# Whole float32 scores for the first batch, and GpSimd for the token differences of layer 2, in an attention and two-layer kernel

## The chip, the cores and the metric

The kernel runs on one core of a Trainium2 chip. The metric is device time in microseconds (us) from the profiler's clock. Five engines work side by side, each with its own queue of instructions in a fixed order: TensorE (PE; its weight loads are shown as PEld), VectorE (DVE), ScalarE (ACT), GpSimd (POOL) and SyncE (SP), which here only issues transfers (DMA).

## The reference

```python
scores = (q @ k^T) / 8                          # 4 batches, 8 heads, 576 tokens, 64 wide
scores = where(scores >= max(scores) - tau, scores, -1e9)
attn = softmax(scores);  x = (attn @ v), heads side by side      # 2304 x 512
h = x @ w1_in;  x = (h * clip(h + 3, 0, 6) / 6) @ w1_out          # 512 -> 2048 -> 512
h = x @ w2_in;  out = (h - tanh(h)) @ w2_out                      # 512 -> 2048 -> 512
```

All inputs and the output are float32. The threshold keeps only scores within tau = 0.02 of a row's maximum, so scores have to be nearly as exact as float32.

## The kernel before

**Products.** TensorE's fast formats carry fewer bits than float32. The kernel therefore splits each float32 operand into a high and a low part and multiplies the parts, in float32r (written fp32r; the profile shows its matmuls as f32) for attention and layer 1 and in float16 for layer 2.

**Attention.** The work is cut into 144 units, 36 for each batch. Most units are 128 queries of one head against all 576 keys; per pair of heads one leftover unit holds the last 64 queries of both heads (576 = 4 x 128 + 64). For a unit `softmax` (line 662) issues the scores into a bank of PSUM (ring `R_s`, two banks), the row maximum on VectorE (L683), the exponential on ScalarE (L685), and the mask times exponential on VectorE (L694), which is the last reader of the bank. Then the result is split into two float16 parts (L699 ScalarE, L705 GpSimd), transposed by a DMA (L708), and four units later multiplied with v (L731).

**Scores with parts.** `k_round` (line 564) transposes k (L561, leftover rows L577). ScalarE writes the high part of one head into rows 0 to 63 of a tile `ks` and of the other head into rows 64 to 127 (L584); VectorE subtracts and writes the low parts into the other half (L586). So the 128 rows of one head hold its high and low parts, one above the other. For q each raw block stands twice side by side in `qr` (a copy by GpSimd, L554), so that its transpose is the same 64 rows twice; ScalarE makes the high part (L591) and VectorE the low part (L593), in the tile `q`, or `qs` for leftover queries. A unit's scores are then, for the high and the low part of q, two matmuls of 288 keys each, four in all, which add up all four products of parts. A leftover unit has two heads and eight matmuls; zeros in `qs` keep the heads apart.

**Weights.** While batch 0 runs, the first half of layer 1's weights is brought from 64-bit form to parts: sixteen pieces, each with a load (L406, L411), a ScalarE step (L414), four VectorE steps (L418, L420, L423, L426), ScalarE's high part (L448) and GpSimd's low part (L451). The pieces are called `ai` and `ao` when they go into matmuls.

**Layers.** Layer 1 takes each batch in two parts (`layer1`, line 819; matmuls at L489 and L850), between the attention units of later batches; its second half of hidden columns follows after all attention, from about 485 us (`hidden`, L489 with tiles `xh`, `bw`). Layer 2 starts at about 720 us. It multiplies blocks of tokens by blocks of weights in a seven-product scheme (Strassen-Winograd), which needs differences of token blocks. `tokens` (line 1315) loads a pair of blocks (L1322), makes four differences T1 to T4 for each of four pairs and one, T5, for the single last block (L1351, 17 in all), and splits each piece into two float16 parts (L1274 ScalarE, L1276 VectorE). It is called once for each pair, in the first of four rounds; later rounds use the same pieces.

**Order.** Every instruction is a task with an engine, an estimated duration and a priority (`add`). `Plan.issue` (line 103) runs a list schedule with these durations, and the order in which it starts the tasks is the order of each engine's queue. A different duration or engine in one place can therefore change the order elsewhere. The transfers are tasks as well, on SyncE's queue.

Of the kernel before, what the change touches and what calls it, by code (L numbers as in the profile page):

```python
# [9 lines left out]
F32 = mybir.dt.float32  # L10
# [5 lines left out]
ACTF = mybir.ActivationFunctionType  # L16
# [14 lines left out]
class Buf:  # L31


    def __init__(self, ring, prev):
        self.ring, self.prev, self.users, self.writers = ring, prev, [], []
        self.tile, self.slot, self.ends = None, None, []

    @property
    def t(self):
        if self.tile is None:  # L40
            self.tile = self.ring.make() if self.slot is None else self.ring.make(self.slot)
        return self.tile


# [156 lines left out]
def attention_moe_moe_kernel(  # L201
# [29 lines left out]
    nc = tc.nc  # L231
    B, H, S, D = q.shape
# [5 lines left out]
    NC = S // 128  # L238
    SM = NC * 128
    LF = S - SM  # L240
    NP = H // 2
    NT = B * S
    SH = S // 2
    ORDER = [0, 2, 1, 3]
    scale = 1.0 / float(D) ** 0.5
# [10 lines left out]
    add = plan.add  # L256

    LAG = 4
    STEP, SLOW, KNEE = 3.0, 0.8, 4
    LK, LQ, LV, LD = 5, 3, 1, 4  # L260
    XL, FO = 1, 7
# [3 lines left out]
    PVK, GK, RK = -4.0, -6.0, -1.0  # L265
# [9 lines left out]
    ST, SB, CS = 4.0, 2.0, 0.0  # L275
# [11 lines left out]
    tau_b = const.tile([128, 4], F32, name="tau_b")  # L287
# [233 lines left out]
    def load_q_left(b, half, key):  # L521

        t = QL[b, half] = R_ql.new()
        hs = slice(half * NP, (half + 1) * NP)
        for r in range(2):
            add("dma", 0.65, key, lambda r=r: nc.sync.dma_start(
                out=t.t[:, :, r, :], in_=q[b, hs, SM:S, :].rearrange("h p d -> p h d")), w=[t], xfer=0.37, slack=SB)

    def load_k(b, j, key):
        t = KR[b, j] = R_kr.new()  # L530
        add("dma", 0.6, key, lambda: nc.sync.dma_start(
            out=t.t, in_=k[b, 2 * j:2 * j + 2, 0:SM, :].rearrange("h (p c) d -> p h c d", c=NC)), w=[t], xfer=0.88, slack=SB)

# [11 lines left out]
    def load_q(b, g, j, key, eng="dma"):  # L545

        t = QR[b, g, j] = R_qr.new()
        queue = nc.sync if eng == "dma" else nc.scalar
        for i in range(2):
            add(eng, 0.47, key, lambda i=i: queue.dma_start(  # L550
                out=t.t[:, i, :, 0, :],
                in_=q[b, 2 * j + i, 0:SM, :].rearrange("(p c) d -> p c d", c=NC)[:, 2 * g:2 * g + 2, :]), w=[t], xfer=0.37, slack=SB)
        copy = lambda r: t.t[:, :, :, r, :].rearrange("p h c d -> p (h c) d")
        add("pool", 0.5, key + 4, lambda: nc.gpsimd.tensor_copy(copy(1), copy(0)), r=[t], w=[t])  # L554

    def transposes(ps, srcs):

# [6 lines left out]
    def k_round(b, j, part, key):  # L564

        if part == 0:
            KS[b, j] = R_k.new()
        ks, tp, kr, kl = KS[b, j], R_tp.new(), KR[b, j], KL[b]
        half = (slice(0, 64), slice(64, 128))
        n = (SM // 2, LF)[part]  # L570

        def tr():
            if part == 0:
                transposes(tp.t, [(kr.t[:, i, c:c + 2, :], 0) for i in range(2) for c in (0, 2)])
            else:
                for i in range(2):
                    nc.tensor.transpose(tp.t[0:64, i * LF:(i + 1) * LF], kl.t[:, 2 * j + i, :], ident[0:LF, 0:LF])  # L577

        add("pe", 2 * n * 0.00085, key, tr, r=[kr] if part == 0 else [kl], w=[tp, ks])
        for x in range(2 - part):  # L580
            cols = slice(x * n, (x + 1) * n) if part == 0 else slice(SM, S)
            out = lambda up, cols=cols: ks.t[half[up], :, cols]
            src = lambda x=x: tp.t[half[x], 0:2 * n].rearrange("p (i n) -> p i n", i=2)
            hi = add("act", t_act(2 * n), key + RK, lambda x=x, out=out, src=src: nc.scalar.activation(  # L584
                out=out(x), in_=src(), func=ACTF.Copy), r=[tp], w=[ks])
            add("dve", t_dve(2 * n), key + RK, lambda x=x, out=out, src=src: nc.vector.tensor_tensor(  # L586
                out=out(1 - x), in0=src(), in1=out(x).bitcast(F32), op=ALU.subtract), r=[tp], w=[ks], after=[hi])
# [8 lines left out]

    def q_round(b, g, j, key):

        qr, tp, qt = QR[b, g, j], R_tp.new(), R_q.new()
        add("pe", 4 * 0.11, key, lambda: transposes(  # L600
            tp.t, [(qr.t[:, i, c, :, :], 0) for i in range(2) for c in range(2)]), r=[qr], w=[tp, qt])
        q_split(qt, tp, lambda x: qt.t[:, x], 256, key)
        QT[b, g, j] = qt

    def q_left_round(b, j, key):

        ql, tp, qt = QL[b, 2 * j // NP], R_tp.new(), R_qs[j % 2].new()
        add("pe", 2 * 0.06, key, lambda: transposes(
            tp.t, [(ql.t[:, (2 * j + i) % NP, :, :], LF) for i in range(2)]), r=[ql], w=[tp, qt])
        q_split(qt, tp, lambda x: qt.t[:, x].rearrange("p (i n) -> p i n", n=LF)[:, 0:3:2, :], LF, key)  # L610
        QT[b, "l", j] = qt
# [50 lines left out]
    def softmax(u, key):  # L662
# [8 lines left out]
        s = lambda: ps.t[:, :, 0:SH]  # L671
        ex = lambda: e.t[:, n, :].rearrange("p (a s) -> p a s", a=2)

        def scores():
            ops = [(queries(b, g, j, x, c, part), KS[b, j].t[:, x % 2]) for x in hs for part in range(2)]
            for i, (l, ks) in enumerate(ops):
                for half in range(2):
                    nc.tensor.matmul(  # L678
                        ps.t[:, half, 0:SH], l, ks[:, half * SH:(half + 1) * SH], start=i == 0, stop=i == len(ops) - 1,
                    )  # L680

        add("pe", 0.53 * len(hs), key, scores, r=[KS[b, j], QT[b, g if h is not None else "l", j]], w=[ps])
        add("dve", 0.69, key, lambda: nc.vector.tensor_reduce(  # L683
            out=z.t[:, 0:1], in_=s(), axis=AX.XY, op=ALU.max, negate=True), r=[ps], w=[z])
        exp = add("act", 0.66, key, lambda: nc.scalar.activation(  # L685
# [179 lines left out]
    with tc.manual_schedule():  # L865
# [94 lines left out]
        start = 0.0  # L960
# [353 lines left out]
        def tokens(p, key, after_y, after):  # L1314
# [26 lines left out]
            def make(name, key):  # L1341

                for o, a, b in sums:
                    if o == name and o not in made:
                        made.add(o)
                        make(a, key)
                        make(b, key)
                        t = R_c.new()
                        src[o] = ((lambda t=t: t.t.rearrange("p (k n) -> p k n", k=2)), t)
                        (fo, bo), (fx, bx), (fy, by) = src[o], src[a], src[b]  # L1350
                        add("dve", t_dve(2 * n), key, lambda: nc.vector.tensor_tensor(  # L1351
                            out=fo(), in0=fx(), in1=fy(), op=ALU.subtract), r=[bx, by], w=[bo], after=after, slack=CL)

            four = lambda i: x.t[:, i, 0:2].rearrange("p a (k n) -> p (a k) n", k=2)
# [242 lines left out]
```

## Time and profile before

| | us |
|---|---|
| median of 3 runs | 1088.65 (1088.2 to 1093.36) |
| the profiled execution | 1088.51 |
| its span, first to last instruction | 1086.7 |
| around the span | 1.8 |
| TensorE busy in the span | 1015.0 (93%) |
| VectorE busy | 847.6 (78%) |
| ScalarE busy | 718.6 (66%) |
| GpSimd busy | 339.0 (31%) |

A share of the whole span is a mean over stages with different limits, so the stage tables below say more than this table does. The granted TensorE clock is given as a share of 2.4 GHz; it has two levels, 0.5 (1.2 GHz) and 1.0.

### The profile page before, as it was taken

To read this page: it belongs to the slowest core of one execution; us is meant where nothing else is said; L and a number is where in the kernel's file an instruction comes from. 1 tells how busy PE (TensorE), PEld (TensorE's weight loads), DVE (VectorE), ACT (ScalarE), POOL (GpSimd) and SP (SyncE) were. 2 spreads that over 40 slices of the span, in tenths; PEclk is the share of its full clock that TensorE was granted. 3 is DMA by queue.
4 is the path that set the end of the run, shared out by engine and by line. 5 is a ranking of instruction groups with operands and counts; after the bars stand their busy time and mean duration, and the time that the engine had idled before them with its cause. 6 is when DMAs were issued, how large, how long until landed. Compare 5 with 4: busy or idle time off the path is not lost.

```text
span 1086.7 us, 23294 instructions
## 1 busy us (share of the span) xinstructions
PE 1015.0 (93%) x8984; PEld 838.6 (77%) x8984; DVE 847.6 (78%) x1630; ACT 718.6 (66%) x1312; POOL 339.0 (31%) x353
## 2 busy tenths in 40 slices
PE   5668799999999899988999999999999999999998
PEld 4557788998999799978988888876676666666664
DVE  5889977687869788758797778889976796784564
ACT  6867979687967786645675566756755675574332
POOL 2656757666855675623000000000001111121000
PEclk8668899999999989998999999999999999999999
DMA  7899688967899989978657755432333866573335
GB/s 184 165 222 213 132 159 182 196 132 158 187 181 192 205 175 216 219 159 261 201 173 257 253 199 185 165 108 97 107 117 118 208 131 117 126 127 51 87 92 142
DMA packets 285007, 179.27 MB, mean 165 GB/s; under 512 B 202976, under 2 KB 257760, under 8 KB 284896
## 3 DMA queue, kind: packets, MB, share of 16 engines
q1 hardware_dynamic: 279088, 168.07, 61.0%
q0 software_dynamic: 5184, 9.44, 6.5%
q8 instruction: 71, 1.16, 0.5%
q14 instruction: 40, 0.33, 0.1%
q10 hardware_dynamic: 624, 0.26, 0.1%
HBM read 89.13 MB, written 46.14 MB: 124 GB/s over the span
## 4 chain that ended last, share of the span: by engine, by line
PE 58%; DVE 4%; ACT 1%; DMA 1%; issue 0%; SPq 0%; ACTq 0%; DVEq 0%
PE ya L489 24%; PE m L489 16%; PE h L489 10%; PE m L850 3%; PE s L678 2%; PE tp L731 1%; DMA y<-y 1%; PE h L850 1%; PE m L476 0%; DVE x L1276 0%; DMA st<-in_moe_w_in_dram 0%; DVE xh L1048 0%; DVE t L803 0%; PE tp L561 0%; DVE y L1175 0%
## 5 line engine op out<-in xcount | busy, mean ns | idle before, releaser
L705 POOL TENSOR_TENSOR pp<-e,pp 128x128 f16<-128x128 f32 (+3 forms) x156 | 181.1, 1182 | 120.3 <-issue 54.1
L489 PE MATMUL ya<-wo,g 128*128 128x512 f16 x864 | 205.4, 379 | 1.0 <-DVE g L813 0.6
L489 PEld LDWEIGHTS <-wi 128*128 128x128 f16 x1536 | 150.0, 98 | 40.4
L1416 POOL DMA_DIRECT2D po<-o x36 | 31.2, 876 | 459.7 <-ACT o L1410 459.7
L489 PEld LDWEIGHTS <-g 128*128 128x128 f16 x864 | 84.1, 98 | 79.3 <-DVE g L813 1.1
L683 DVE TENSOR_REDUCE z<-s 128x1 f32<-128x576 f32 x144 | 107.9, 753 | 45.4 <-PE s L678 44.7
L694 DVE SCALAR_TENSOR_TENSOR e<-s,z,e 128x576 f32<-128x576 f32 x144 | 115.8, 811 | 22.1 <-ACT e L685 17.1
L678 PE MATMUL s<-ks,q 128*128 128x288 f32 x512 | 105.9, 337 | 20.9 <-DVE e L694 20.1
L685 ACT ACTIVATE e<-s,z 128x576 f32<-128x576 f32 x144 | 105.0, 739 | 26.6 <-DVE z L683 20.3
L489 PE MATMUL m<-xT,ai 128*128 128x256 f32 (+1 forms) x720 | 112.8, 301 | 1.8 <-DVE st L426 0.6
L678 PEld LDWEIGHTS s<-ks,q 128*128 128x128 f32 x512 | 82.4, 212 | 29.4 <-DVE e L694 13.4
L489 PEld LDWEIGHTS m<-xT,ai 128*128 128x128 f32 x720 | 99.3, 190 | 3.7 <-DVE st L426 1.1
L489 PE MATMUL ya<-g,bo 128*128 128x256 f16 x864 | 101.1, 273 | 0.5 <-DVE g L813 0.5
L731 PE MATMUL tp<-vt,pt 128*128 128x65 f16 (+1 forms) x2240 | 88.4, 199 | 8.5 <-ACT q L591 2.4
L489 PE MATMUL m<-x,wi 128*128 128x256 f16 x768 | 95.2, 273 | 0.0
L731 PEld LDWEIGHTS <-pt 128*128 128x128 f16 (+1 forms) x2240 | 79.8, 104 | 16.7 <-DMA pt<-pp 6.0
L1381 ACT ACTIVATE t<-t,hid_s 128x512 f32<-128x512 f32 x72 | 51.6, 718 | 62.0 <-DVE t L1372 61.4
L489 PEld LDWEIGHTS <-bo 128*128 128x128 f16 x864 | 84.1, 98 | 10.6 <-issue 0.9
L489 PEld LDWEIGHTS <-bw 128*128 128x128 f16 x864 | 84.1, 98 | 10.4 <-issue 0.4
L813 DVE SCALAR_TENSOR_TENSOR g<-g,t 128x512 f16<-128x512 f16 x108 | 73.8, 686 | 20.7 <-ACT g L809 20.2
L809 ACT ACTIVATE g<-t 128x512 f16<-128x512 f32 x108 | 67.0, 624 | 33.7 <-DVE t L1383 26.0
L699 ACT ACTIVATE pp<-e 128x1152 f16<-128x1152 f32 (+1 forms) x80 | 85.1, 1064 | 5.0 <-DVE e L694 4.7
(177 smaller groups left out, 1878.0 us busy)
## 6 DMA issues: line engine op xcount, KB each, us to landing
st<-in_moe_w_in_dram SPq DMA_DIRECT2D x40, 512.0 KB, 5.0
st<-in_moe_w_out_dram SPq DMA_DIRECT2D x40, 512.0 KB, 4.4
xf<-xs SPq DMA_DIRECT2D x18, 512.0 KB, 5.2
y<-y SPq DMA_DIRECT2D x18, 512.0 KB, 3.8
po<-o POOLq DMA_DIRECT2D x36, 256.0 KB, 4.2
xs<-xT SPq DMA_DIRECT2D x8, 640.0 KB, 4.9
y<-ys SPq DMA_DIRECT2D x9, 512.0 KB, 5.9
po<-o SPq DMA_DIRECT2D x18, 256.0 KB, 2.0
```

The lines of the kernel that those rows point to most:

```text
L489: nc.tensor.matmul(ps, l[a], r[b], start=first and t == 0 and i == 0, stop=last and t == 2 and i == n - 1,)
L678: nc.tensor.matmul(ps.t[:, half, 0:SH], l, ks[:, half * SH:(half + 1) * SH], start=i == 0, stop=i == len(ops) - 1,)
L683: add("dve", 0.69, key, lambda: nc.vector.tensor_reduce(out=z.t[:, 0:1], in_=s(), axis=AX.XY, op=ALU.max, negate=True), r=[ps], w=[z])
L685: exp = add("act", 0.66, key, lambda: nc.scalar.activation(out=ex(), in_=s(), func=ACTF.Exp, bias=z.t[:, 0:1]), r=[ps, z], w=[e])
L694: add("dve", 0.74, key, lambda: nc.vector.scalar_tensor_tensor(out=ex(), in0=s(), scalar=z.t[:, 1:2], in1=ex(), op0=ALU.is_ge, op1=ALU.mul ...
L699: high = add("act", t_act(w * S, sbuf=True), key, lambda: nc.scalar.activation(out=pp.t[:, 0:w, 0:S], in_=e.t[:, 0:w, :], func=ACTF.Copy), ...
L705: add(eng, dur, key, lambda src=src, dst=dst, queue=queue: queue.tensor_tensor(out=pp.t[:, 0:w, dst], in0=e.t[:, 0:w, src], in1=pp.t[:, 0: ...
L731: nc.tensor.matmul(pv.t[0:m, w_ * (D + 1):(w_ + 1) * (D + 1)], pt.t[:, n, blk, rows], vv, start=o == 0, stop=o == len(ops) - 1)
L809: hi = add("act", t_act(n, sbuf=True), key, lambda: nc.scalar.activation(out=gh(), in_=t(), func=ACTF.Copy, scale=GS2 if far else 1.0), r= ...
L813: go = lambda: nc.vector.scalar_tensor_tensor(out=gl(), in0=gh(), scalar=1.0 / GS2, in1=t(), op0=ALU.mult, op1=ALU.subtract)
L850: prev = [add("pe", t_mm(n, 1), kd, lambda p=p, l=l, r=r, m=m, s=s, ps=ps: nc.tensor.matmul(ps.t[:, 0:n], W["o", m].t[:, l, s], r[m].t[:, ...
L1381: add("act", t_act(2 * NB, sbuf=True, scalars=True), key, lambda: nc.scalar.activation(out=s_(), in_=h.t, func=ACTF.Tanh, scale=c), r=[h], ...
```

## The change

For batch 0 (`WHOLE = (0,)`) q and k are no longer split. One ScalarE copy takes the transposed k of a head pair into a float32 tile, head 0 in rows 0 to 63 and head 1 in rows 64 to 127; q likewise, with the scale. A unit's scores are two float32 matmuls of 288 keys, with 64 rows of q and k. For a leftover unit the two heads' queries stand in different rows and columns of the tile `q`, the rest of which VectorE clears, and the 128 rows of both heads are multiplied at once. The loads of k and of the raw q put the two heads' 64 columns side by side for each block, so that one transpose serves both heads; k comes in two transfers in place of one, the leftover q in one in place of two, and the doubling copies of q are not made. In `tokens` the differences move from VectorE to GpSimd.

```diff
+    WHOLE = (0,)
@@ load_q_left, load_k, load_q
+        if b in WHOLE:
+            add("dma", 0.65, key, lambda: nc.sync.dma_start(
+                out=t.t.rearrange("p h r d -> p (h r) d")[:, 0:NP, :], in_=q[b, hs, SM:S, :].rearrange("h p d -> p h d")),
+                w=[t], xfer=0.37, slack=SB)
+            return
...
+        for i in range(2 if b in WHOLE else 0):
+            add("dma", 0.5, key, lambda i=i: nc.sync.dma_start(
+                out=cells(t)[:, :, i, :], in_=k[b, 2 * j + i, 0:SM, :].rearrange("(p c) d -> p c d", c=NC)), w=[t], xfer=0.44, slack=SB)
...
+        if b in WHOLE:
+            for i in range(2):
+                add(eng, 0.47, key, lambda i=i: queue.dma_start(
+                    out=pairs_of(t)[:, :, i, :],
+                    in_=q[b, 2 * j + i, 0:SM, :].rearrange("(p c) d -> p c d", c=NC)[:, 2 * g:2 * g + 2, :]), w=[t], xfer=0.37, slack=SB)
+            return
@@ new
+    def pairs_of(t):
+        return t.t.rearrange("p i c r d -> p (i c r d)")[:, 0:4 * D].rearrange("p (c i d) -> p c i d", c=2, i=2)
+    def cells(t):
+        return t.t.rearrange("p i c d -> p (i c d)").rearrange("p (c i d) -> p c i d", c=NC, i=2)
+    def whole(ring, tag):
+        t = ring.new()
+        t.make = lambda: at_p.tile([128, 2, S] if tag == "ks" else [128, 2, 2, 256], F32, tag=tag, name=tag + "w", bufs=ring.n)
+        return t
@@ k_round
+        if b in WHOLE:
+            w = (SM, LF)[part]
+            def turn_whole():
+                if part:
+                    nc.tensor.transpose(tp.t[:, 0:LF], kl.t[:, 2 * j:2 * j + 2, :].rearrange("p i d -> p (i d)"), ident[0:LF, 0:LF])
+                for x, c in enumerate(() if part else ORDER):
+                    nc.tensor.transpose(tp.t[:, x * 128:(x + 1) * 128], cells(kr)[:, c].rearrange("p i d -> p (i d)"), ident)
+            add("pe", w * 0.00085, key, turn_whole, r=[kl if part else kr], w=[tp, ks])
+            add("act", t_act(w), key + RK, lambda: nc.scalar.activation(
+                out=ks.t[:, 0, part * SM:part * SM + w], in_=tp.t[:, 0:w], func=ACTF.Copy), r=[tp], w=[ks])
+            return
@@ q_round, q_left_round
+            add("pe", 2 * 0.11, key, lambda: [nc.tensor.transpose(
+                tp.t[:, c * 128:(c + 1) * 128], pairs_of(qr)[:, c].rearrange("p i d -> p (i d)"), ident) for c in range(2)],
+                r=[qr], w=[tp, qt])
+            add("act", t_act(256, scalars=True), key + RK, lambda: nc.scalar.activation(
+                out=qt.t[:, 0, 0], in_=tp.t[:, 0:256], func=ACTF.Copy, scale=tau_b[:, 2:3]), r=[tp], w=[qt])
...
+            clear = add("dve", 0.1, key, lambda: nc.vector.memset(qt.t[:, 0, 1, 0:2 * LF], 0.0), w=[qt])
+            add("pe", 0.06, key, lambda: nc.tensor.transpose(...), r=[ql], w=[tp, qt])
+            for i in range(2):
+                half = slice(i * 64, i * 64 + 64)
+                add("act", t_act(LF, scalars=True), key + RK, lambda i=i, half=half: nc.scalar.activation(
+                    out=qt.t[half, 0, 1, i * LF:(i + 1) * LF], in_=tp.t[half, 0:LF], func=ACTF.Copy, scale=tau_b[half, 2:3]), r=[tp], w=[qt], after=[clear])
@@ softmax
+        def scores_whole():
+            rows = slice(0, 128) if h is None else slice(h % 2 * 64, h % 2 * 64 + 64)
+            qt, ks = QT[b, g, j].t, KS[b, j].t
+            l = qt[:, 0, 1, 0:2 * LF] if h is None else qt[rows, 0, 0, c % 2 * 128:c % 2 * 128 + 128]
+            for half in range(2):
+                nc.tensor.matmul(
+                    ps.t[:, half, 0:SH], l, ks[rows, 0, half * SH:(half + 1) * SH], start=True, stop=True)
-        add("pe", 0.53 * len(hs), key, scores, r=[...], w=[ps])
+        add("pe", 0.98 if b in WHOLE else 0.53 * len(hs), key, scores_whole if b in WHOLE else scores, r=[...], w=[ps])
@@ tokens
-                        add("dve", t_dve(2 * n), key, lambda: nc.vector.tensor_tensor(
+                        add("pool", t_pool(2 * n), key, lambda: nc.gpsimd.tensor_tensor(
                             out=fo(), in0=fx(), in1=fy(), op=ALU.subtract), r=[bx, by], w=[bo], after=after, slack=CL)
```

## Rows read from the trace of the kernel before

**Rows 1.** Busy time by stage: PE, PEld, DVE, ACT, POOL; clock, DMA share, GB/s

```profile
10.00:97.00 87.00, 59.89 (x458) 50.24 (x457) 75.21 (x126) 66.83 (x128) 51.70 (x47) 0.67 0.87 195
97.00:136.00 39.00, 31.33 (x367) 28.59 (x364) 37.27 (x65) 34.82 (x76) 27.61 (x28) 0.91 0.78 159
136.00:480.00 344.00, 329.46 (x3705) 312.97 (x3702) 263.41 (x514) 259.18 (x496) 213.88 (x217) 0.99 0.87 180
...
700.00:760.00 60.00, 57.06 (x450) 43.56 (x448) 55.34 (x119) 41.33 (x68) 0.00 (x0) 1.00 0.29 102
760.00:1087.00 327.00, 321.91 (x2158) 210.81 (x2155) 230.28 (x424) 173.22 (x295) 31.25 (x36) 1.00 0.50 118
```

**Rows 2.** Waits of PE in the first 97 us: total, times, longest

```profile
PE s L678 <- DVE e L694: 13.5, 12, 2.6
```

**Rows 3.** Timeline of the start: start, length, instruction, idle before it

```profile
5.13 1.09 PE L561 MATMUL tp<-ident,kr 128*128 128x128 f32 x4 [5.13 <-DMA kr<-in_k_dram]
...
6.26 1.20 ACT L584 ACTIVATE ks<-tp 64x512 fp32r<-64x512 f32 x2 [3.21 <-PE tp L561]
...
7.49 1.39 DVE L586 TENSOR_TENSOR ks<-tp,ks 64x512 fp32r<-64x512 f32 x2 [2.94 <-ACT ks L584]
...
10.51 1.31 PE L678 MATMUL s<-ks,q 128*128 128x288 f32 x4
```

**Rows 4.** Transfers issued in the first 97 us: size, median us to landing

```profile
kr<-in_k_dram SPq DMA_DIRECT2D x7, 256.0 KB, 4.2
...
qr<-in_q_dram SPq DMA_DIRECT2D x16, 64.0 KB, 3.8
```

**Rows 5.** Groups on DVE by form, first 140 us: busy us, mean ns

```profile
L586 DVE TENSOR_TENSOR ks<-tp,ks 64x512 fp32r<-64x512 f32 x12 | 8.3, 689 | 4.1 <-ACT ks L584 3.8
L593 DVE SCALAR_TENSOR_TENSOR q<-tp,tau_b,q 128x512 fp32r<-128x512 f32 x10 | 7.4, 745 | 0.7 <-ACT q L591 0.6
...
L586 DVE TENSOR_TENSOR ks<-tp,ks 64x128 fp32r<-64x128 f32 x6 | 1.7, 284 | 0.7 <-ACT ks L584 0.5
L593 DVE SCALAR_TENSOR_TENSOR qs<-tp,tau_b,qs 128x128 fp32r<-128x128 f32 x4 | 1.4, 341 | 0.0
```

**Rows 6.** Timeline of PE: scores and transposes at both clock levels

```profile
20.55 1.30 PE L678 MATMUL s<-ks,q 128*128 128x288 f32 x4 [0.95 <-DVE e L694]
...
93.44 2.29 PE L678 MATMUL s<-ks,qs 128*128 128x288 f32 x8
...
100.57 0.66 PE L561 MATMUL tp<-ident,qr 128*128 128x128 f32 x4
...
102.17 0.79 PE L678 MATMUL s<-ks,q 128*128 128x288 f32 x4 [0.94 <-DVE e L694]
```

**Rows 7.** Groups on PE by form, first 140 us: line 628

```profile
L628 PE MATMUL tp<-vs,ones 128*128 128x1 f32 x10 | 2.2, 288 | 2.4 <-ACT vt L626 2.0 <-DVE m L418 0.4
```

**Rows 8.** Groups on PE by form, first 97 us: scores of full units

```profile
L678 PE MATMUL s<-ks,q 128*128 128x288 f32 x96 | 28.9, 450 | 11.3 <-DVE e L694 10.9
```

**Rows 9.** Busy time in two stretches, columns as in rows 1

```profile
91.00:94.00 3.00, 2.86 (x10) 2.18 (x11) 3.00 (x5) 2.62 (x5) 0.87 (x2) 0.50 1.19 272
105.00:125.00 20.00, 19.03 (x229) 17.76 (x230) 19.10 (x35) 18.13 (x44) 15.64 (x17) 1.00 0.93 194
```

**Rows 10.** Line 1351 alone: ns min/median/max, first and last start

```profile
L1351 DVE TENSOR_TENSOR c<-y x9: 673/681/691, 714.9 to 771.0; 128x512 f32<-128x512 f32 x9
```

**Rows 11.** Groups on POOL by form, first 140 us: the low parts of weights

```profile
L451 POOL TENSOR_TENSOR ai<-st,ai 128x512 fp32r<-128x512 f32 x8 | 10.4, 1304 | 4.6 <-ACT ai L448 4.6
```

**Rows 12.** Timeline, 490 to 497 us: DVE beside POOL

```profile
491.25 0.75 DVE L1128 SCALAR_TENSOR_TENSOR bw<-st,wmax,bw 128x512 f16<-128x512 f32 x1
...
494.52 2.45 POOL L816 TENSOR_TENSOR gl<-t,gh 128x320 fp32r<-128x320 f32 x2 [7.76 <-ACT gh L809]
...
495.14 1.09 DVE L1128 SCALAR_TENSOR_TENSOR bw<-st,wmax,bw 128x512 f16<-128x512 f32 x1 [0.19 <-ACT bw L1126]
```

**Rows 13.** Timeline of PE, 712 to 765 us: layer 2's first piece

```profile
720.53 1.47 PE L489 MATMUL m<-x,wi 128*128 128x256 f16 x12
```

More of the change, by code (lines that the diff above doesn't have):

```diff
@@ L35, in __init__ @@
         self.ring, self.prev, self.users, self.writers = ring, prev, [], []
-        self.tile, self.slot, self.ends = None, None, []
+        self.tile, self.slot, self.ends, self.make = None, None, [], None
     @property
@@ L40, in t @@
         if self.tile is None:
-            self.tile = self.ring.make() if self.slot is None else self.ring.make(self.slot)
+            self.tile = self.make() if self.make else self.ring.make() if self.slot is None else self.ring.make(self.slot)
         return self.tile
@@ L566, in k_round @@
         if part == 0:
-            KS[b, j] = R_k.new()
+            KS[b, j] = whole(R_k, "ks") if b in WHOLE else R_k.new()
         ks, tp, kr, kl = KS[b, j], R_tp.new(), KR[b, j], KL[b]
@@ L570, in k_round @@
         n = (SM // 2, LF)[part]
+        if b in WHOLE:
+            w = (SM, LF)[part]
[7 more added lines that the diff above has]
+                out=ks.t[:, 0, part * SM:part * SM + w], in_=tp.t[:, 0:w], func=ACTF.Copy), r=[tp], w=[ks])
+            return
         def tr():
@@ L597, in q_round @@
     def q_round(b, g, j, key):
+        if b in WHOLE:
+            qr, tp, qt = QR[b, g, j], R_tp.new(), whole(R_q, "q")
+            add("pe", 2 * 0.11, key, lambda: [nc.tensor.transpose(
[3 more added lines that the diff above has]
+                out=qt.t[:, 0, 0], in_=tp.t[:, 0:256], func=ACTF.Copy, scale=tau_b[:, 2:3]), r=[tp], w=[qt])
+            QT[b, g, j] = qt
+            return
         qr, tp, qt = QR[b, g, j], R_tp.new(), R_q.new()
@@ L605, in q_left_round @@
     def q_left_round(b, j, key):
+        if b in WHOLE:
+            ql, tp, qt = QL[b, 2 * j // NP], R_tp.new(), QT[b, 1, j]
+            clear = add("dve", 0.1, key, lambda: nc.vector.memset(qt.t[:, 0, 1, 0:2 * LF], 0.0), w=[qt])
+            add("pe", 0.06, key, lambda: nc.tensor.transpose(
+                tp.t[:, 0:LF], ql.t.rearrange("p h r d -> p (h r d)")[:, 2 * j % NP * D:(2 * j % NP + 2) * D], ident[LF:2 * LF, LF:2 * LF]),
+                r=[ql], w=[tp, qt])
+            for i in range(2):
+                half = slice(i * 64, i * 64 + 64)
+                add("act", t_act(LF, scalars=True), key + RK, lambda i=i, half=half: nc.scalar.activation(
+                    out=qt.t[half, 0, 1, i * LF:(i + 1) * LF], in_=tp.t[half, 0:LF], func=ACTF.Copy, scale=tau_b[half, 2:3]), r=[tp], w=[qt], after=[clear])
+            QT[b, "l", j] = qt
+            return
         ql, tp, qt = QL[b, 2 * j // NP], R_tp.new(), R_qs[j % 2].new()
@@ L680, in scores @@
                     )
-        add("pe", 0.53 * len(hs), key, scores, r=[KS[b, j], QT[b, g if h is not None else "l", j]], w=[ps])
+        add("pe", 0.98 if b in WHOLE else 0.53 * len(hs), key, scores_whole if b in WHOLE else scores, r=[KS[b, j], QT[b, g if h is not None else "l", j]], w=[ps])
         add("dve", 0.69, key, lambda: nc.vector.tensor_reduce(
```

## The prediction

> **What bounds the kernel now.** I read the stage table first [rows 1], because the change touches two places only. From 760 us on TensorE is busy for 321.9 of 327 us at full clock: nothing off TensorE can be worth much there. In the 60 us from 700 to 760, where layer 2 starts, 60 - 57.1 = 2.9 us are idle. From 136 to 480 us TensorE is busy 329.5 of 344 us at a granted clock of 0.99. The opening is different. Between 10 and 97 us, which is batch 0 before the first matmul of layer 1, TensorE is busy 59.9 of 87 us, and that at a mean clock of 0.67, while VectorE is busy 75.2 (86%), ScalarE 66.8 and the DMA engines 0.87. VectorE is the fullest engine, but not a full one. The view of TensorE's waits for the first 97 us says how it acts on TensorE [rows 2]: 13.5 us in 12 waits of the score matmuls for line 694, the masked exponentials that free a score bank. Between 97 and 136 us VectorE is busy 37.3 of 39 us and TensorE 31.3, so 7.7 us of TensorE are idle there.
>
> The order of instructions on each engine is fixed when the program is built, and nothing in it refers to the time on the chip. So a microsecond gained before 136 us is kept to the end as long as TensorE stays full behind it, and a microsecond of TensorE work added after 97 us is mostly paid.
>
> **The start (term A).** The timeline of the start [rows 3] is a chain: transposes of k until 6.2, two ScalarE copies until 7.5, two VectorE subtractions until 8.9, then q's and the leftover rows of k, and the first scores at 10.51. With whole numbers one copy of k (0.6) and one of q (taken as 0.5) end near 7.4, the leftover's transpose and copy near 8: about -2.4 us. Against it stands the load of k, now two issues with short runs. A 256 KB load of k lands in 4.2 us and a 64 KB load of q, whose runs are as short, in 3.8 [rows 4], so halves of 128 KB should land at much the same time. I take -2.0.
>
> **VectorE, batch 0.** Removed: 8 subtractions of 64x512 at 0.689, 4 of 64x128 at 0.284, 8 of q at 0.745 and 4 of the leftover q at 0.341 [rows 5]: 5.5 + 1.1 + 6.0 + 1.4 = 14.0 us. Added: four clears of 128 elements, bounded below by nothing and above by the 0.284 of a small subtraction; I take 0.17, 0.7 in all. Net -13.3 us, of which 2.4 lie before 10 us (already in A), about 10 between 10 and 97, and 1 after. ScalarE loses four of its eight 512-wide copies of k and half the width of q's; GpSimd loses the eight copies that doubled q. Neither is the fullest engine, so these count as nothing; if VectorE were no cover, ScalarE's 66.8 us would be the next limit.
>
> **TensorE, batch 0.** Before, a unit's scores are four streams of 288 columns: hi and lo of k lie one above the other in 128 rows, so two passes (hi and lo of q) by two halves form all four partial products. Such a unit takes 1.30 us at the low clock and 0.79 at the high one [rows 6]. After, k fills only 64 rows and nothing is stacked. No row shows a wide float32 product; the nearest is line 628, where 5 float32 products stand as 10 matmuls and 10 weight loads [rows 7], that is two of each per product. Low end: the two products of a unit are then four streams as now, and cost nothing more. High end: the four partial products, no longer stacked, need four streams for each half, eight in all. That has a row: the leftover units already run eight streams, in 2.29 us at the low clock [rows 6]; at the high clock, by the same ratio, 1.3 to 1.4. I take the high end, since four partial products in 64 rows cannot be had in fewer streams: +0.95 us a unit at the low clock, +0.5 at the high one. The Trainium skill (FP8 and Floating Point Precision, TensorE Precision Notes) counts a true float32 product as four passes through the array, which would give the same eight streams; no run here shows it yet. There are 32 such units, 24 of them before 97 us (96 matmuls, four a unit [rows 8]); the four leftover units have eight streams before and after. Savings: two transposes instead of four for each of eight q rounds, half of 1.09 us at the low clock and of 0.66 at the high one [rows 3, 6], so 0.5 or 0.3 each.
>
> **10 to 97 us (term B).** If VectorE's occupancy sets the stretch, 65.2 us of work at the same 86% take 75.5 us: -11.5. If TensorE sets it, 59.9 + 24 x 0.95 - 7 x 0.5 = 79 us, at the same 86%, take 92 us: +5. Which is nearer depends on the clock. In the rows [rows 9] TensorE was still at 0.50, its low level of 1.2 GHz, from 91 to 94 us after 80 us of broken work, and from 105 to 125 us, after layer 1 had kept it busy since 97, it held 1.00, that is 2.4 GHz. At 1.00 the added streams cost 12 us instead of 23, and old work shrinks too. Longer score bursts should bring the high level more often than now. I lean to VectorE's side and take -6.0. What is late next is then the score chain itself (scores, maximum, exponential, mask) with two banks.
>
> **97 to 136 us (term C).** Eight more units cost 8 x 0.5 = 4 us at the high clock; below, nothing, since 7.7 us are idle there, mostly because line 694 stands on VectorE behind steps of the weight splitting, some of which move ahead into the room that opens before 97 us. I take +1.5.
>
> **Layer 2's differences (term D).** 17 subtractions of 0.681 us, nine of the form shown and eight alike [rows 10], leave VectorE: 11.6 us from 715 us on; in the 60 us from 700 VectorE is busy 55.3. On GpSimd the nearest row is the subtraction of weights, the same 512 elements, 1.304 us [rows 11]. GpSimd is idle then (0.00 in rows 1), so 17 x 1.3 = 22 us are covered by an empty engine. They are queued before the accumulating stores of later blocks only. For the first pair of blocks the chain of two differences ends at 714.9 + 2 x 1.4 = 717.7, its two halves are made some 1.5 us later, and the matmuls of layer 2 start at 720.5 [rows 13] with a piece that needs no difference. If that cover were gone, 2 x 0.6 = 1.2 us of delay would show once. At most 2.9 us of idle TensorE can be won; I take -1.0, bounds -2 and +3.
>
> The rule that speaks against this edit: rows first. A subtraction of line 1128, 0.75 us alone, took 1.09 us while GpSimd was subtracting [rows 12]. The Trainium skill (GPSIMD Engine Reference, Specifications) says that GpSimd shares its SBUF interfaces with VectorE and contends with VectorE instructions that have two SBUF inputs; the trace agrees, with that 0.34 us. Its section Engine selection would leave elementwise work with VectorE. By row alone 17 x 0.34 = 5.8 us of VectorE time come back, less than the 11.6 removed.
>
> **Sum.** -2.0 - 6.0 + 1.5 - 1.0 = -7.5 us. The profiled execution took 1088.5 (its span 1086.7 and 1.8 around it), the median is 1088.65: 1081.0 us.
>
> **Rivals.**
> 1. VectorE's time is returned in full: A -2.4, B -11.5, C 0, D -2: -16, so 1072.5. For it: 86% and 37.3 of 39 us. Against it: the waits of VectorE would have to shrink in proportion, and the DMA share would go from 0.87 to 1.0.
> 2. Something else sets the opening: DMA at 0.87 with transposes by DMA between every pair of units, or the score chain. Then A -2, B 0, C +1.5, D 0: 1088. For it: ScalarE has hardly less work, and TensorE's score bursts grow.
> 3. TensorE takes VectorE's place at the low clock (slower): B +5, C +4, A -2, D 0: +7, so 1095.5. With the other terms as given the change turns slower by 0.5% once B passes +3.4, which is 90.4 us at 86%, so once TensorE's work in the stretch passes 78 us; the streams at the low clock make 79. For it: the stretch ran at a mean of 0.67 although TensorE was busy 69% of it. Against it: a TensorE that is so full has held the high level in every later stage.
> 4. By the rule on shared interfaces, GpSimd's subtractions stretch both engines when layer 2 starts and its first pieces wait: D +3 instead of -1, so 1085. Against it: 5.8 us against 11.6, and TensorE waited for VectorE little there. The page named above is the GPSIMD Engine Reference.
> 5. The float32 products cost only the low end, four streams: then B lies at its VectorE end, as in rival 1; it is counted there.
>
> **Chances and range.** Forecast 0.40 (own range 1075 to 1087), rival 1 0.19, rival 2 0.22, rival 3 0.12, rival 4 0.07. The 80% range goes from the price of rival 1 to nearly that of rival 3: 1071 to 1094. A change of 0.5% (5.4 us) is about what a measurement tells from none: faster than 1083.2, slower than 1094.1. The forecast falls on the fast side in about three of four of its cases, rival 1 always, rivals 2 and 4 rarely: 0.40 x 0.75 + 0.19 + 0.03 = 0.52. Slower: most of rival 3 and a little of rival 2, 0.12. The rest, 0.36, is no change.
>
> **What would show it.** The first scores should start near 8.5 us instead of 10.51. Line 678's successor should show four matmuls a unit in batch 0, together 2.2 us at the low clock or 1.3 at the high one; if they take 1.3 and 0.8, the high end was wrong. The granted clock from 10 to 97 us should be above 0.67. The first matmul of layer 1 should start near 89 us instead of 97.1, and batch 1 near 129 instead of 136. The differences should stand on GpSimd at 1.3 to 1.8 us each, and TensorE's idle time between 700 and 760 should not be above 2.9 us. The prediction is wrong if the first matmul of layer 1 does not move, if the new order of the instructions opens a gap between 136 and 520 us, or if a wait for GpSimd's differences stands ahead of layer 2.

## The result and the profile after

The changed kernel takes 1105.17 us (median of 6 runs, 1102.61 to 1107.67), the kernel before beside it 1089.33 (6 runs, 1088.2 to 1093.36): ratio 1.014, 95% interval 1.0117 to 1.0162. It is 15 us slower where 7.5 us faster was forecast, and lies above the range (1071 to 1094). The profiled execution took 1104.4 us, its span is 1102.6.

Line numbers have moved: the scores of batch 0 are now line 741 (678 before, 748 for the other batches), the masked exponentials 764 (694), the prepared pieces of layer 2 line 1346 (1276), the differences 1421 (1351), the gate's last product 883 (813).

The stage table of the changed kernel, columns as in [rows 1]:

```profile
10.00:97.00 87.00, 72.95 (x383) 46.76 (x382) 59.76 (x100) 58.88 (x117) 44.53 (x37) 0.97 0.76 166
97.00:136.00 39.00, 35.56 (x295) 27.43 (x295) 35.23 (x58) 30.89 (x69) 24.46 (x26) 0.89 0.86 200
136.00:480.00 344.00, 326.16 (x3632) 307.79 (x3633) 265.85 (x516) 262.31 (x503) 219.19 (x222) 0.98 0.85 178
700.00:760.00 60.00, 55.27 (x458) 44.38 (x456) 54.16 (x104) 40.47 (x68) 14.30 (x9) 1.00 0.33 114
760.00:1103.00 343.00, 336.30 (x2264) 221.00 (x2261) 243.40 (x442) 182.63 (x311) 42.83 (x44) 1.00 0.49 118
```

Against [rows 1] the opening is turned round. From 10 to 97 us TensorE is busy 72.95 us instead of 59.89, with 383 matmuls instead of 458, and VectorE 59.76 instead of 75.21: VectorE lost its load and, in the same time, did less of the rest too (100 instructions, 126 before). The waits of the scores for line 764 fell only from the 13.5 us of [rows 2] to 10.5:

```profile
PE s L741 <- DVE e L764: 10.5, 9, 2.3
```

The start went as forecast, and better; the timeline, to set beside [rows 3]:

```profile
5.66 1.08 PE L606 MATMUL tp<-ident,kr 128*128 128x128 f32 x4 [0.77 <-DMA kr<-in_k_dram]
6.79 0.87 ACT L609 ACTIVATE ksw<-tp 128x512 f32<-128x512 f32 x2 [1.15 <-PE tp L606]
...
7.60 4.15 PE L741 MATMUL s<-ksw,qw 64*128 64x288 f32 x8
```

The first scores start at 7.60 us instead of 10.51. But eight score matmuls, two units, take 4.15 us. The groups of TensorE by form for the first 97 us, to set beside [rows 8]:

```profile
L741 PE MATMUL s<-ksw,qw 64*128 64x288 f32 x90 | 49.0, 704 | 10.6 <-DVE e L764 8.9 <-DVE vs L694 1.6
```

90 matmuls take 49.0 us, where 96 took 28.9. A mean of 704 ns is the price at the low level, and here the clock column of the stage table misleads. It says 0.97 for 10 to 97 us, but this trace holds no granted clock before 88.4 us, and the table counts a stretch without one as full (in [rows 1] that is so only up to 14.8 us). The durations tell the level. TensorE's timeline around the first rise:

```profile
84.96 2.26 PE L741 MATMUL s<-ksw,qw 128*128 128x288 f32 x4 [1.56 <-DVE e L764]
87.01 1.64 PE L801 MATMUL tp<-vt,pt 128*128 128x65 f16 x28
88.57 1.24 PE L741 MATMUL s<-ksw,qw 64*128 64x288 f32 x4
...
92.27 2.28 PE L741 MATMUL s<-ksw,qw 64*128 64x288 f32 x4 [0.32 <-DVE e L764]
...
100.26 2.29 PE L741 MATMUL s<-ksw,qw 64*128 64x288 f32 x4
102.47 1.72 PE L801 MATMUL tp<-vt,pt 128*128 128x65 f16 x28
104.01 2.32 PE L490 MATMUL m<-xT,ai 128*128 128x256 f32 x12
```

and three shorter stretches of the stage table:

```profile
8.00:36.00 28.00, 25.41 (x86) 15.27 (x85) 17.03 (x33) 21.01 (x42) 10.06 (x9) 1.00 0.80 185
...
88.00:97.00 9.00, 7.78 (x59) 5.38 (x57) 8.51 (x15) 7.59 (x17) 7.27 (x7) 0.71 0.76 185
97.00:104.00 7.00, 7.00 (x43) 4.72 (x43) 5.94 (x9) 2.58 (x5) 2.53 (x3) 0.50 0.55 137
```

A unit takes 1.24 us where the clock is high (88.57) and 2.28 where it is at 0.50 (92.27). It took 2.26 to 2.29 in all of 8 to 88 us, two in a row 4.15 to 4.18, so TensorE stood at 1.2 GHz throughout, though it was busy 25.41 of the 28 us from 8 on. Before the change the clock had risen six times by 90 us, for 24 us in all. Here it rose at 88.4, behind a unit of leftovers on 128 rows and the 128-row products that follow, fell behind units on 64 rows, and rose again once layer 1's matmuls on 128 rows had begun. In scores alone, the first experiment below, the same unit and products brought no rise; the first came at 108.2, behind layer 1's first matmuls.

Where the time goes, from the timelines (start in us):

| | before | after | scores alone | same order, 128 rows |
|---|---|---|---|---|
| first scores | 10.51 | 7.60 | 7.84 | 8.06 |
| first matmul of layer 1 | 97.1 | 104.0 | 105.2 | 87.3 |
| its second half | 136.7 | 147.1 | 148.9 | 131.6 |
| first of layer 1's second-hidden matmuls | 524.5 | 537.5 | 539.8 | 522.0 |
| last of them | 714.4 | 727.0 | 729.3 | 711.5 |
| first piece of layer 2 | 720.5 | 735.8 | 735.5 | 717.6 |
| end | 1086.7 | 1102.6 | 1101.5 | 1084.1 |

(The last two columns are experiments, below.) The changed kernel is 6.9 us late at the first matmul of layer 1; it loses 3.5 more by the second half of layer 1's first chunk, 2.6 more up to the first second-hidden matmul, and 2.6 between layer 1's last matmuls and layer 2 (6.2 us before, 8.8 now). That last place, in the timeline of the changed kernel:

```profile
725.10 1.75 DVE L1346 SCALAR_TENSOR_TENSOR wo<-c,wmax,wo 128x512 f16<-128x512 f32 x1
...
726.26 3.39 POOL L1421 TENSOR_TENSOR c<-y,c 128x512 f32<-128x512 f32 x2
726.77 1.75 DVE L883 SCALAR_TENSOR_TENSOR g<-g,t 128x512 f16<-128x512 f16 x1
...
728.58 2.67 PE L490 MATMUL ya<-g,bo 128*128 128x256 f16 x23 [1.19 <-DVE g L883]
728.69 2.04 DVE L1346 SCALAR_TENSOR_TENSOR x<-y,ypow,x 128x1024 f16<-128x1024 f32 x1
...
732.52 0.69 DVE L883 SCALAR_TENSOR_TENSOR g<-g,t 128x512 f16<-128x512 f16 x1
732.54 0.27 PE L490 MATMUL ya<-g,bo 128*128 128x256 f16 x1 [1.29 <-ACT g L879]
733.26 2.67 PE L490 MATMUL ya<-g,bo 128*128 128x256 f16 x23 [0.46 <-DVE g L883]
735.77 1.47 PE L490 MATMUL m<-x,wi 128*128 128x256 f16 x12
```

Beside a subtraction of GpSimd line 883 takes 1.75 us here, alone 0.69 (in three later places beside one, 0.68 to 0.96). TensorE waits 1.19, 1.29 and 0.46 us for the gate's parts, where it waited 0.51 in all before, and layer 2's first piece [rows 13] starts behind that.

Added up over all 17 subtractions, the VectorE operations beside them took 11.1 us longer than the same forms take alone (13 of them by 0.28 to 1.08 us each), about as much as the 11.6 us that the move took off VectorE. GpSimd was busy 26.2 us with the subtractions.

### The profile page after: what moved, and what is told of

Read it like the earlier page. It is cut to its first block, busy times and chain, and to the rows that moved or that the text cites. A ratio compares the mean times of both kernels' runs of the same rounds, so it can differ in the third digit from the quotient of the medians.

```text
span 1102.6 us, 23172 instructions
## 1 busy us (share of the span) xinstructions
PE 1044.0 (95%) x8944; PEld 842.4 (76%) x8944; DVE 838.7 (76%) x1593; ACT 714.8 (65%) x1312; POOL 359.9 (33%) x362
## 4 chain that ended last, share of the span: by engine, by line
PE 52%; DVE 4%; ACT 1%; DMA 1%; issue 1%; POOL 0%; DVEq 0%; ACTq 0%
PE ya L490 24%; PE m L490 14%; PE h L490 10%; PE m L920 1%; DVE t L1442 1%; PE m L477 1%; DMA pt<-pp 1%; PE h L920 1%; PE tp L801 1%; DVE t L1453 0%; DVE g L883 0%; DVE x L1346 0%; DVE t L873 0%; POOL pp L775 0%; PE m L470 0%
## 5 line engine op out<-in xcount | busy, mean ns | idle before, releaser
L755 ACT ACTIVATE e<-s,z 128x576 f32<-128x576 f32 x144 | 105.2, 738 | 32.1 <-DVE z L753 20.2
L1421 POOL TENSOR_TENSOR c<-y 128x512 f32<-128x512 f32 x9 | 13.1, 1476 | 225.0 <-DVE t L873 195.4
L741 PE MATMUL s<-ksw,qw 64*128 64x288 f32 (+1 forms) x144 | 67.8, 620 | 14.8 <-DVE e L764 13.2
```

The source lines that it names most:

```text
L741: nc.tensor.matmul(ps.t[:, half, 0:SH], l, ks[rows, 0, half * SH:(half + 1) * SH], start=True, stop=True)
L755: exp = add("act", 0.66, key, lambda: nc.scalar.activation(out=ex(), in_=s(), func=ACTF.Exp, bias=z.t[:, 0:1]), r=[ps, z], w=[e])
```

## The experiments

"Scores alone" is the changed kernel with the differences back on VectorE.

**1. Scores alone.**

```diff
-add("pool", t_pool(2 * n), key, lambda: nc.gpsimd.tensor_tensor(
+add("dve", t_dve(2 * n), key, lambda: nc.vector.tensor_tensor(
```

> The whole float32 scores of batch 0 alone; layer 2's differences stay on VectorE. Theory (TensorE takes VectorE's place at the low clock): most of the 16 us stay, 1101 to 1103 us, with the first layer 1 matmul near 104 us and the first layer 2 piece near 733. Rival (the differences on GpSimd are the larger part): 1094 or less.

Measured: 1104.64 us, ratio 1.013 (1.0106 to 1.0153), first rise of the clock at 108.2 us. The scores carry nearly all of the loss.

**2. Differences alone.** The kernel before, with the opposite edit at line 1351.

> The differences of layer 2 on GpSimd alone; batch 0 as before. Theory (VectorE and GpSimd hold each other up, so VectorE loses more than it is relieved of): 1091 to 1093 us, all of it between 715 and 785 us. Rival (the move is neutral, as TensorE is full): 1088 to 1090.

Measured: 1096.18 us, ratio 1.0053 (1.0034 to 1.0073), more than the theory expected. TensorE's timeline there:

```profile
713.86 2.78 PE L489 MATMUL h<-xh,bw 128*128 128x256 f16 x24
717.59 0.27 PE L489 MATMUL ya<-g,bo 128*128 128x256 f16 x1 [0.94 <-ACT g L809]
720.21 8.05 PE L489 MATMUL ya<-g,bo 128*128 128x256 f16 x47 [2.36 <-DVE g L813]
728.10 1.47 PE L489 MATMUL m<-x,wi 128*128 128x256 f16 x12
```

TensorE waits 0.94 and 2.36 us. Within the second wait, at 719.1, the granted clock falls for 6.8 us (0.72 on the mean of 716 to 728 us), and 47 matmuls take 8.05 us that took 2.78 + 2.67 before. 11.7 us lie between layer 1's last second-hidden matmul and layer 2, 6.2 before: 5.5 us more. So this edit alone costs 5.8 us by the ratio, and 2.6 us of it lie in the clock that fell in this short wait. (The profiled execution is 7.7 us longer than that of before; 2.0 of these lie ahead of 524 us, where the order is still the same, and are scatter.) The move also changed the order of the VectorE and ScalarE instructions around the first blocks; no run separates what that adds from what the collisions cost.

**3. Scores on 128 rows.** The queries of each head are written to a tile of their own, with zeros in the other head's rows, by a second ScalarE copy with a scale of zero in those rows.

```diff
-add("act", ..., out=qt.t[:, 0, 0], in_=tp.t[:, 0:256], scale=tau_b[:, 2:3])
+for i in range(2):
+    add("act", ..., out=qt.t[:, i, 0], in_=tp.t[:, 0:256], scale=hid_s[:, 0, 0, i:i + 1])
...
-rows = slice(0, 128) if h is None else slice(h % 2 * 64, h % 2 * 64 + 64)
+rows = slice(0, 128)
```

> As e1, but q stands in 128 rows with zeros for the other head, so that each score matmul uses all 128 rows of k and q; two ScalarE copies of q in place of one. The streams cost TensorE the same. Theory (64 rows are what keeps the clock low): the clock rises within the first 40 us, the mean from 10 to 97 us is 0.65 or more, and the time falls to 1090 to 1096 us. Rival (the float32 format keeps it low, whatever the rows): first rise near 88 us as in the changed kernel, 1101 us or more.

Measured: 1102.81 us, ratio 1.0109 (1.0081 to 1.0137). The clock rises from 11.9 us on (0.82 from 10 to 97), as the theory had it, and layer 1 starts at 90.1 us; but the time is the rival's. Between 118 and 147 us the lead is lost, and the first second-hidden matmul comes 14.8 us later than before the change. TensorE there:

```profile
127.00 2.53 PE L742 MATMUL s<-ksw,qw 128*128 128x288 f32 x8 [1.72 <-DVE e L765]
132.42 3.38 PE L802 MATMUL tp<-vt,pt 128*128 128x65 f16 x56 [2.88 <-DVE ks L627]
```

It waits 2.88 us for line 627 of batch 1's keys, which stands on VectorE behind steps of the weight splitting, and VectorE in its turn then waits 5.95 us for ScalarE's part of the next unit. That points to the order of the instructions, so runs 6, 10 and 11 try others.

**4. Rows or format.** Batch 0 in float32r on 64 rows, each matmul twice, so that a unit has four streams of 288 columns as in the kernel before.

```diff
-t.make = lambda: at_p.tile([128, 2, S] ..., F32, ...)
+t.make = lambda: at_p.tile([128, 2, S] ..., F32R, ...)
...
+for twice in range(2):
     for half in range(2):
-        nc.tensor.matmul(..., start=True, stop=True)
+        nc.tensor.matmul(..., start=twice == 0, stop=twice == 1)
```

> As e1, but the whole tiles are float32r and each of the two matmuls of a unit is made twice, so four streams as before the change; the low parts of q and k are left out and the scores doubled. VectorE's relief without the price of float32. Theory: the first layer 1 matmul comes near 90 us and the time is 1080 to 1086 us. Rival (VectorE's relief is worth nothing, the score chain sets the pace): 1088 to 1091. If 64 rows alone keep the clock low, this shows here as well: no rise before 80 us.

Measured: 1089.43 us (10 runs, 1083.26 to 1091.13), ratio 0.9983 (0.9962 to 1.0005). The first scores:

```profile
7.97 2.26 PE L742 MATMUL s<-ksw,qw 64*128 64x288 f32 x8
```

Eight matmuls, two units, take 2.26 us, little more than half of the 4.15 us in float32, and still at the low level. The first rise comes at 88.5 us. So the float32 format isn't what holds the clock down. The median is the rival's: with half the streams, and with VectorE's relief, the low clock costs nothing against before. Three of the ten runs took 1083.3 to 1084.1 us, as the theory had it, and seven 1088.5 to 1091.1; the profile is of one of the three, and what parts the two groups is open.

**5. Matmuls on 128 rows put between.** Scores alone, and before each unit two bfloat16 matmuls of 128 rows whose result the scores overwrite. The order on every engine is kept.

```diff
+for _ in range(2): nc.tensor.matmul(ps.t[:, 0, 0:256], ident.bitcast(BF16)[:, 0:128],
+                                    ident.bitcast(BF16)[:, 0:256], start=True, stop=True)
```

> Edit to the kernel with the whole scores alone: ahead of each unit's score matmuls of batch 0 two more matmuls of 128 rows and 256 columns in bfloat16, whose result the scores overwrite; every engine keeps its order, only TensorE gets 72 instructions more. Theory (64 rows hold the granted clock low, and TensorE at the low level sets the opening): the clock rises before 25 us, the four matmuls of a unit take 1.24 us instead of 2.28, layer 1's first matmul comes near 90 to 95 us (105.2 without the fillers, 90.1 with scores on 128 rows), and the median falls by 5 to 14 us from 1104.6, to 1091 to 1100. Rival (the clock is a by-product, TensorE's work or the order of the work sets the opening): the fillers are 72 x 0.21 = 15 us more work at the low level, layer 1's first matmul comes at 112 to 120, and the median is 1112 to 1120.

Measured: 1114.14 us, ratio 1.0224 (1.0182 to 1.0265). The theory failed as put: two fillers of 0.3 us beside 2.28 us of 64-row scores bring no rise before 100 us.

```profile
20.98 0.58 PE L740 MATMUL s<-ident 128*128 128x256 bf16 x2 [0.53 <-DVE e L764]
21.50 2.29 PE L742 MATMUL s<-ksw,qw 64*128 64x288 f32 x4
```

As a load test it speaks all the same: the 50 fillers ahead of layer 1, 15.1 us of TensorE, move its first matmul by 11.6 us (105.2 to 116.8). For the most part TensorE's work sets the opening here.

**6, 7. The planner's price.** The change told the planner 0.98 us for a unit's scores. Run 6 is run 3 with 1.25, run 7 is scores alone with 2.3.

```diff
-add("pe", 0.98 if b in WHOLE else 0.53 * len(hs), key, scores_whole ...
+add("pe", 2.3 if b in WHOLE else 0.53 * len(hs), key, scores_whole ...
```

> Edit to the kernel with scores on 128 rows: the planner is told 1.25 us for a unit's whole scores, which they take at the high level, instead of 0.98. Theory (that kernel reached layer 1 at 90.1 us and lost its lead between 118 and 147 us to an order planned with too low a price): the stretch from unit 30 to unit 35, 29 us there and 17 in the run with four streams of float32r, falls below 22 us, batch 0 ends by 135, and the median is 1083 to 1093. Rival (the stall has a cause of its own, such as the two ScalarE copies in place of one for each pair of heads, or VectorE's random generation put ahead of batch 1's keys): unit 35 stays at 143 to 149 and the median at 1099 to 1105.

> Edit to the kernel with the whole scores alone: the planner is told 2.3 us for a unit's whole scores, what they take at the low level, instead of 0.98. Theory (TensorE at the low level sets the opening whatever the order): 36 units x 2.28 us = 82 us of scores in the first 105 us leave little to win; first rise of the clock not before 85 us, layer 1's first matmul between 98 and 110, median 1097 to 1106. Rival (an order planned with a price of less than half is what costs): layer 1's first matmul near 97, where it was before the change, median 1086 to 1092.

Measured: run 6 1091.94 us, ratio 1.0015 (0.9996 to 1.0034), 11 us under run 3; the last maximum of batch 0 comes at 137.2 us (147.1 in run 3; by 135 was expected), so the order was the cause of that stall. Layer 1 itself starts later than in run 3, at 95.4 us. Run 7 1103.44 us, ratio 1.0113 (1.0069 to 1.0157), first rise at 85.5, layer 1 at 95.1, ahead of the 98 to 110 expected, but its second half only at 146.8. At the low clock the true price buys next to nothing.

**8. Differences on GpSimd, all but the first pair's.**

```diff
+eng, queue, dur = ("pool", nc.gpsimd, t_pool(2 * n)) if p else ("dve", nc.vector, t_dve(2 * n))
...
```

> Edit to the kernel before: the differences of layer 2's token blocks go to GpSimd for all pairs of blocks but the first, 13 of 17 subtractions. Theory (the cost of that part lies where layer 1 ends: the first pair's four subtractions hold up VectorE's last gate operations of layer 1, TensorE idles and its clock falls): the stretch from layer 1's last second-hidden matmul to layer 2's first piece is 6.1 to 6.5 us as before (11.7 with all 17), and the median is within 3 us of 1089. Rival (every subtraction costs about alike through the lock): 13/17 of the 6.9 us, a median near 1094.5.

Measured: 1094.09 us, ratio 1.0035 (1.0016 to 1.0054). The stretch into layer 2 is 6.2 us again, as the theory had it, but the time lies between the two: 3.8 us by the ratio, where the theory allowed 3 and the rival had 5.3. Layer 2 itself takes 371.0 us instead of 366.2. ScalarE and TensorE:

```profile
734.56 0.72 ACT L1274 ACTIVATE xs<-c,ypow 128x512 f16<-128x512 f32 x1 [1.95 <-POOL c L1352]
...
736.47 0.61 PE L489 MATMUL ya<-wo,g 128*128 128x512 f16 x2 [1.73 <-ACT g L809]
```

Here ScalarE stands 1.95 us in front of a piece whose difference GpSimd makes in 1.79 instead of 0.68 us, with the gate's activations queued behind it; TensorE waits 1.73 us, and the clock falls (0.84 from 734 to 745, 1.00 before). Spared in one place, the edit costs in another.

**9. The same order on 128 rows.** Scores alone, one line changed.

```diff
-rows = slice(0, 128) if h is None else slice(h % 2 * 64, h % 2 * 64 + 64)
+rows = slice(0, 128)
```

> Edit to the kernel with the whole scores alone: each score matmul of batch 0 reads all 128 rows of its tiles in place of one head's 64, so that it adds both heads' scores (it leaves out the parting of the heads). Every instruction of every engine stands where it stood, with the same columns. Theory (64 rows hold the granted clock low): the clock rises before 25 us, the four matmuls of a unit take 1.2 us whenever it is high, the mean granted clock in the records of 10 to 97 us is 0.75 or more by durations, layer 1's first matmul comes at 88 to 95 us (105.2 with 64 rows), and what is kept to the end is 5 to 16 us: a median of 1089 to 1100. Rival (the float32 scores or the order hold it low; the run with other tiles and copies for 128 rows differed for another reason): the first rise comes after 85 us, layer 1's first matmul at 100 or later, median within 4 us of 1104.6.

Measured: 1087.98 us, ratio 0.9973 (0.9953 to 0.9993), against 1.013 with 64 rows: 17 us from the rows alone, with every instruction in its old place. The score group of the first 97 us in scores alone:

```profile
L741 PE MATMUL s<-ksw,qw 64*128 64x288 f32 x88 | 48.7, 715 | 10.3 <-DVE e L764 8.6 <-DVE vs L694 1.6
```

the same group in this run:

```profile
L741 PE MATMUL s<-ksw,qw 128*128 128x288 f32 x108 | 42.1, 527 | 19.5 <-DVE e L764 19.0 <-DVE vs L694 0.3
```

and its stretch of the stage table:

```profile
10.00:97.00 87.00, 62.60 (x485) 44.69 (x485) 71.97 (x120) 67.75 (x137) 52.64 (x44) 0.84 0.91 202
```

108 matmuls take 42.1 us where 88 took 48.7. The clock rises at 11.4 us, in the second unit, and layer 1 starts at 87.3 us; VectorE is the fullest engine again (72 of 87 us). The 715 ns of scores alone is the low level, 527 a mix of both. At one and the same level the rows don't change the price: a unit takes 1.24 us at the high level in this run as on 64 rows (88.57 above), and 2.26 at the low one (84.96 above, 128 rows) against 2.28. So the gain is the clock's.

**10, 11, 12. Price and order on 128 rows.** Run 10 is run 3 with a price of 1.6. Run 11 has the order of run 9: the planner sees the two copies as one task.

```diff
-for i in range(2):
-    add("act", ..., lambda i=i: nc.scalar.activation(...), r=[tp], w=[qt])
+add("act", ..., lambda: [nc.scalar.activation(...) for i in range(2)], r=[tp], w=[qt])
```

Run 12 is run 11 with the differences on GpSimd.

> Edit to the kernel with scores on 128 rows: the planner is told 1.6 us for a unit's whole scores, what they take at a granted clock of 0.8, in place of 0.98 (1102.81 us) and 1.25 (1091.94 us). Theory (the order was worth 11 us there because the price was too low, and the mean price is the right one): unit 35 no later than 137 us, median 1083 to 1092. Rival (each price gives another order, and what it is worth is chance): median 1092 to 1104.

> Edit to the kernel with scores on 128 rows and two ScalarE copies of each pair's queries: the planner is told of the two copies as one task at the price of one, so that every instruction stands where it stands in the run that adds both heads' scores (1087.98 us), with 16 ScalarE copies of 0.45 to 0.48 us more, and the scores are the reference's. Theory (order and rows are all that counts, and ScalarE, busy 68 of 87 us there, has room for 7 us): layer 1's first matmul at 87 to 92 us, median 1084 to 1091. Rival (the second copy stands in the way of the exponentials of the units): layer 1's first matmul after 95 us, median 1095 to 1104, as in the run at 1102.81.

> The same kernel with the differences of layer 2's token blocks on GpSimd: the whole change, with scores on 128 rows. Theory (GpSimd's subtractions hold up VectorE's operations on two SBUF tiles wherever they fall together, TensorE then idles and its clock may fall; this costs 2.5 to 7 us in any order of the attention): 2.5 to 7 us above the run beside it without them. Rival (what they cost hangs on the order of the attention, as the 0.5 us between the whole change and the whole scores alone would have it): within 2 us of the run beside it.

Measured: run 10 1094.02 us, ratio 1.003 (1.0012 to 1.0048): the mean price is not the best one, as the rival said. Run 11 1090.34, ratio 1.0003 (0.9986 to 1.0019). It has 8 ScalarE copies more than run 9 (16 in all, not 16 more); the clock rises at 11.9 us, zeros in the other head's rows or not; layer 1 starts at 88.8 us, 8.3 ahead of before, but 0.3 of it is left at 524 us. Run 12 1093.18, ratio 1.0027 (1.0014 to 1.0041), 2.8 us above run 11. Of these versions none beats the kernel before.

## Why the prediction was wrong

**The step that failed: term B, its clock.** "Longer score bursts should bring the high level more often than now", and on it "I lean to VectorE's side and take -6.0". The bursts grew longer, and the high level did not come at all until 88 us: the change halves the rows of a score matmul, and on 64 rows the clock stayed low. Run 9 against scores alone shows that it is the rows (17 us, all else in its place), run 4 that it is not the format, run 7 that it is not the price. Over all traces, the first rise comes at 85.5 to 108.2 us with scores on 64 rows (the changed kernel, runs 1, 4, 5, 7) and at 11.4 to 39.8 us with scores on 128 (the kernel before, runs 2, 3, 6, 8 to 12). The Trainium skill (TensorE: Matmul & The Clock Gate, The HAM clock gate) has the gate follow how busy the array has been; this trace goes against reading that as busy time, with 25.41 of 28 us and no rise.

**What took its place** is rival 3, TensorE in VectorE's place at the low clock, with the chance of 0.12. Its work was right: 79 us forecast, 72.95 until 97 and 7.00 until 104.0 measured, 80 in 94 us, or 85% where 86% was taken. Its "against it" was the mistake of term B once more: later stages held the high level with matmuls on 128 rows. And its price, +7, was too small: B +5 and A -2 would make the first matmul of layer 1 3 us late, and it came 6.9 late; the rest of the 15.9 us between the profiled spans lies mostly in terms C and D and in batches 1 to 3, where rival 3 had 4, 0 and nothing.

**Term A** (-2.0): the first scores came 2.9 us earlier. Right as a step, but nothing of it is left at the first matmul of layer 1.

**The streams.** The high end was right: 2.28 us at the low level and 1.24 at the high one, forecast 2.2 and 1.3. The Trainium skill (FP8 and Floating Point Precision, TensorE Precision Notes) counts four passes for a float32 product; the trace agrees: two units take 4.15 us, and in run 4, with half as many streams, 2.26.

**Term C** (+1.5): +3.5 us, near rival 3's +4. At 104 us TensorE still had units of batch 0 to score.

**"A microsecond gained before 136 us is kept"** did not hold either, and this is a second step that failed: in run 11 the clock rises and layer 1 starts at 88.8 us, where the prediction had 89, and yet the time is 1090.34 and not 1081. The changed kernel loses 2.6 us more between 136 and 524, run 11 loses there 3.1 of the 3.3 us by which it led. Each kernel has an order of its own in batches 1 to 3, since the planner's times for batch 0 move everything behind them; runs 3, 6 and 10, alike but for one price, lie 11 us apart. Part of the small losses is scatter of single executions: run 12, in run 11's order there, takes 1.9 us less for that stretch, and run 2, in the order of the kernel before, 1.4 more than it. The prediction's condition, that TensorE stays full behind the gain, is not met everywhere: from 355 to 400 us TensorE is busy 39.15 us at a mean clock of 0.92 before, and 37.54 at 0.85 in run 11. But run 2 has about as long a time at the low level there. So what in these orders costs was seen only in run 3, and stays open for the others.

**Term D** (-1.0, bounds -2 and +3): the sign was wrong, and rival 4 right in kind. Alone the edit costs 5.8 us (run 2), in the order of run 11 2.8, beside the changed scores 2.6 at its place and 0.5 in the medians (1105.17 against 1104.64); in the profiled executions the changed kernel happens to reach the second-hidden matmuls at 537.5 us, where scores alone, in the same order, needs 539.8. The step that failed was the price of a collision: [rows 12] show 0.34 us on a VectorE operation, which made 5.8 us; here one cost up to 1.08 (line 883: 1.06, from 0.69 to 1.75), and all together 11.1, so that VectorE was hardly relieved. The Trainium skill (GPSIMD Engine Reference, Specifications) names the shared interfaces; the trace agrees, and adds the price. The view of totals (11.6 us off VectorE) said nothing on this; what counted was which operation of the gate is late and that TensorE's clock falls behind it.

## What to carry to other kernels

Before giving up rows of a matmul to save work on another engine, ask what that does to the granted clock as well as to the streams: with VectorE's relief counted in, eight streams on 128 rows cost nothing here (run 9), four on 64 rows cost nothing (run 4), eight on 64 rows cost some 15 us. A stage that ends earlier is not yet a kernel that ends earlier: follow the lead through the later stages. Read the clock from the durations of one known form, not from a column that may have no record. A subtraction moved to an idle GpSimd is paid by VectorE's operations beside it; by these runs it is cheap only where none of them feeds the engine that sets the time.

## What the runs showed of the hardware

TensorE, with scores in float32 on 64 rows and busy 25.41 of 28 us, stayed at 1.2 GHz for 80 us; with the same instructions on 128 rows its clock rose at 11.4 us, and with zeros in half of the rows of q at 11.9 (run 11). With float32r on 64 rows it stayed low as long (88.5 us). Two bfloat16 matmuls of 128 rows and 0.58 us together before each 2.28 us unit brought no rise before 100.1 us.

In run 2 TensorE had held the high level for 201 us; from within the second of two waits, of 0.94 and 2.36 us, it stood at the low one for 6.8 us, and 47 matmuls took 8.05 instead of 5.45 us.

GpSimd's subtraction of 128x512 takes 1.27 us undisturbed and up to 2.28 beside VectorE, and VectorE's product of 128x512 0.69 alone and up to 1.75 beside it: both engines lose.
